# K and V in transfers of four heads, long weight rows, bf16 transposes, output in rows and w2 last: one decode layer on one core

## The chip, the core and the metric

The kernel runs on one core of a Trainium2 chip. Five engines work beside each other, each through its own list of instructions in order: PE (TensorE, matmuls; its weight loads are shown as PEld), DVE (VectorE), ACT (ScalarE), POOL (GpSimd) and SP (SyncE, which here only issues transfers). Sixteen DMA engines move data between HBM and SBUF; PE writes its results to PSUM, from where DVE or ACT copies them. The metric is device time in microseconds (us): the median of several runs. The kernel before takes 142.29 us (three runs, 142.29 to 142.35).

## The reference

A parallel layer for one new token and a batch of two (D = 576). The normalized input goes both through attention over the last 2048 of 8192 cached positions (32 query heads of width 128, 16 heads in the K and V caches, so two query heads share one) and through a dense block with squared ReLU (F = 4608); both results are added to the input.

```python
W = min(4096, max(256, Sk // 4))                       # 2048
q = (x @ wq).reshape(B, 1, 32, 128)
k = jnp.repeat(k_cache[:, :, Sk - W:, :], 2, axis=1)
v = jnp.repeat(v_cache[:, :, Sk - W:, :], 2, axis=1)
p = softmax(einsum(q, k) * 128 ** -0.5)
attn = einsum(p, v).reshape(B, 1, 4096) @ wo
h = xn @ w1 + b1
mlp = where(h > 0, h, 0) ** 2 @ w2 + b2
out = x + attn(xn) + mlp(xn)                           # xn = layernorm(x)
```

All inputs and the output are bf16. K and V of the window are 33.55 MB, wq and wo 4.72 MB each, w1 and w2 5.31 MB each: 53.6 MB are read, and hardly anything is written.

## The kernel before

**Tiles.** K and V come one head of one batch at a time, 512 KB each: `kv_view` (L80) puts 16 consecutive positions into each of the 128 partitions, so a row of a transfer is 4 KB. `issue_wo` (L140) loads two heads' 256 rows of wo with rows of 1152 bytes, and `issue_w2` (L154) 512 rows of w2, mostly as rows of 4608 bytes. wq and w1 come in pieces of 128 rows of 8192 and 9216 bytes, with a remainder of 64 rows folded over all partitions.

**Steps.** The main loop (L407) has 16 steps, one per K/V head, for both batches. `transposes` (L295) views pairs of bf16 columns as f32 and turns them with 8 f32 matmuls of 128 columns against an identity; ACT copies one half of the result to SBUF and DVE the other. Since the pairs are still interleaved after that, the query is first spread into `zq` with a zero in every second place (L280 to L289), and `scores` (L315) makes two accumulating matmuls for each pair. `softmax` (L325) takes the maximum over positions (DVE, then POOL across partitions), subtracts, exponentiates (ACT), sums (DVE, POOL) and inverts. `pv` (L352) runs two steps later, `wo_proj` (L366) three steps later. The output is built transposed: each block of 128 rows of wo or w2 is the stationary operand in five column blocks, with two moving columns (the batch), and all add up in one PSUM tile, `outT_ps`. At the end x and b2 are added (L452), five transposes bring the result into rows (L455), and it is copied and stored.

**Order.** All loads are issued by SP in program order. A list of eight semaphores is used in turn, so the ninth transfer waits for the first to land; beyond that a transfer waits until its buffer is free (ten K and ten V buffers). w1 is loaded in the first steps, w2 and wo are spread over the steps, and the last loads are V of heads 14 and 15, a w2 piece, and wo of heads 13 to 15. Inside a step PE runs transposes, the older `pv`, `scores` of one batch, `wo_proj`, the dense block's matmuls, and `scores` of the other batch; a framework places the waits and shifts some of these.

**Start.** The identities are made on POOL (`make_identity`, lines of `masks.py`), behind four small transfers that POOL issues itself.

Of the kernel before, what the change touches and what calls it, by code (L numbers as in the profile page):

```python
# [9 lines left out]
F32 = mybir.dt.float32  # L10
# [7 lines left out]
def kernel(  # L18
# [50 lines left out]
    ktpool = ctx.enter_context(tc.tile_pool(name="ktpool", bufs=5))  # L69
    wbig = ctx.enter_context(tc.tile_pool(name="wbig", bufs=NFULL))  # L70
    wrem = ctx.enter_context(tc.tile_pool(name="wrem", bufs=2))
    wpool = ctx.enter_context(tc.tile_pool(name="wpool", bufs=3))
    wopool = ctx.enter_context(tc.tile_pool(name="wopool", bufs=6))
    work = ctx.enter_context(tc.tile_pool(name="work", bufs=3))
    keep = ctx.enter_context(tc.tile_pool(name="keep", bufs=5))
# [5 lines left out]
    def kv_view(cache, b, t):  # L81
        return cache[b, t, S0:Sk, :].rearrange("(p j) d -> p j d", p=P)

    k_tiles, v_tiles, wq_tiles, w1_tiles, wo_tiles, w2_tiles = {}, {}, {}, {}, {}, {}
    WBW = max(Hq * Dh, F)

    def issue_k(t, b):
        tl = kpool.tile([P, NJ, Dh], BF16, tag="k_sb", name=f"k_{t}_{b}")
        nc.sync.dma_start(out=tl[:], in_=kv_view(A_k_cache, b, t))
        k_tiles[(t, b)] = tl  # L90

    def issue_v(t, b, pool=None):
        if pool is None:
            tl = vpool.tile([P, NJ, Dh], BF16, tag="v_sb", name=f"v_{t}_{b}")
        else:
            tl = pool.tile([P, NJ, Dh], BF16, tag="k_sb", name=f"v_{t}_{b}")
        nc.sync.dma_start(out=tl[:], in_=kv_view(A_v_cache, b, t))
        v_tiles[(t, b)] = tl

    WRW = max(LQ, L1)  # L100

    def issue_wq(c):
        if c < NFULL:
            tl = wbig.tile([P, WBW], BF16, tag="wbig", name=f"wq_{c}")
            nc.sync.dma_start(out=tl[:, 0:Hq * Dh], in_=A_wq[c * P:(c + 1) * P, :])
        else:
            tl = wrem.tile([P, WRW], BF16, tag="wrem", name="wq_rem")
            nc.sync.dma_start(out=tl[:, 0:LQ],
                              in_=A_wq[NFULL * P:D, :].rearrange("r (s l) -> (r s) l", s=S))
        wq_tiles[c] = tl  # L110

    def issue_w1(c):
        if c < NFULL:
            tl = wbig.tile([P, WBW], BF16, tag="wbig", name=f"w1_{c}")
            nc.sync.dma_start(out=tl[:, 0:F], in_=B_w1[c * P:(c + 1) * P, :])
        else:
            tl = wrem.tile([P, WRW], BF16, tag="wrem", name="w1_rem")
            nc.sync.dma_start(out=tl[:, 0:L1],
                              in_=B_w1[NFULL * P:D, :].rearrange("r (s l) -> (r s) l", s=S))
        w1_tiles[c] = tl  # L120
# [9 lines left out]
    GW = FG * P  # L130

    def piece_permuted(g):
        return (g * GW) // L1 == (g * GW + GW - 1) // L1

    def h_cols(fc):
        g, r = divmod(fc, FG)
        if piece_permuted(g):
            return g * GW + r, FG
        return g * GW + r * P, 1

    def issue_wo(t, split=False):
        h0 = rep * t
        if not split:
            tl = wopool.tile([P, rep, D], BF16, tag="wo_sb", name=f"wo_{t}")
            nc.sync.dma_start(out=tl[:],
                              in_=A_wo[h0 * Dh:(h0 + rep) * Dh, :].rearrange("(r p) n -> p r n", p=P))
            for hh in range(rep):
                wo_tiles[h0 + hh] = (tl, hh)
        else:
            for hh in range(rep):  # L150
                tl = wopool.tile([P, 1, D], BF16, tag="wo_sb", name=f"wo_{t}_{hh}")
                nc.sync.dma_start(out=tl[:, 0, :], in_=A_wo[(h0 + hh) * Dh:(h0 + hh + 1) * Dh, :])
                wo_tiles[h0 + hh] = (tl, 0)

    def issue_w2(m):
        tl = wpool.tile([P, FG, D], BF16, tag="w2_sb", name=f"w2_{m}")
        rows = B_w2[m * GW:(m + 1) * GW, :]
        if piece_permuted(m):
            nc.sync.dma_start(out=tl[:], in_=rows.rearrange("(p r) n -> p r n", r=FG))
        else:  # L160
            nc.sync.dma_start(out=tl[:], in_=rows.rearrange("(r p) n -> p r n", p=P))
        w2_tiles[m] = tl
# [6 lines left out]
    nc.scalar.activation(out=warm[:, 0:1], in_=eps_t[:], func=ACT.Sqrt)  # L169
    issue_wq(0)  # L170
    issue_k(0, 0)
    b1_sb = const.tile([NFC, P], BF16, name="b1_sb")
    nc.gpsimd.dma_start(out=b1_sb[:], in_=B_b1.rearrange("(c p) -> c p", p=P))  # L173
    b1g_sb = const.tile([NMG, GW], BF16, name="b1g_sb")
    nc.gpsimd.dma_start(out=b1g_sb[:], in_=B_b1.rearrange("(g c) -> g c", c=GW))
    b2_sb = const.tile([NCH, OC], BF16, name="b2_sb")
    nfull = D // OC
    nc.gpsimd.dma_start(out=b2_sb[0:nfull, :], in_=B_b2[0:nfull * OC].rearrange("(c p) -> c p", p=OC))
    for c in range(nfull, NCH):
        nc.gpsimd.dma_start(out=b2_sb[c:c + 1, :],  # L180
                            in_=B_b2[ostart[c]:ostart[c] + OC].rearrange("(c p) -> c p", c=1))
    issue_wq(1)
    issue_k(0, 1)
    issue_wq(2)
    issue_k(1, 0)
    issue_wq(3)
    issue_k(1, 1)
    for c in range(4, KC):
        issue_wq(c)

    ident = const.tile([P, P], BF16, name="ident")
    make_identity(nc, ident[:])
    ident_f = const.tile([P, P], F32, name="ident_f")
    make_identity(nc, ident_f[:])
    HP = P // 2
    sel = const.tile([P, 2, P], BF16, name="sel")
    nc.gpsimd.memset(sel[:], 0.0)
    for i in range(2):
        nc.gpsimd.affine_select(
            out=sel[:, i, :].rearrange("p (a u) -> p a u", a=2),  # L200
            in_=sel[:, i, :].rearrange("p (a u) -> p a u", a=2),
            compare_op=ALU.not_equal, fill=1.0, base=-i,
            pattern=[[0, 2], [-2, HP]], channel_multiplier=1,
        )

    outT_ps = psum.tile([OC, NCH, B], F32, tag="outT", name="outT_ps")
    nc.vector.memset(outT_ps[:], 0.0)
# [14 lines left out]

# [5 lines left out]
    NXN = NFULL + S  # L228
    OFF_XN = 0
    OFF_X = OFF_XN + NXN * B  # L230
    PRO_W = OFF_X + NCH * B
    pro_ps = psum.tile([P, PRO_W], BF16, tag="misc", name="pro_ps")
    for c in range(NFULL):
        nc.tensor.transpose(out=pro_ps[:, OFF_XN + c * B:OFF_XN + (c + 1) * B],  # L234
                            in_=xn_sb[:, c * P:(c + 1) * P], identity=ident[:B, :B])
    for sg in range(S):
        c = NFULL + sg
        nc.tensor.transpose(out=pro_ps[:, OFF_XN + c * B:OFF_XN + (c + 1) * B],
                            in_=xr_sb[:, sg, :], identity=ident[:B, :B])
    for c in range(NCH):  # L240
        nc.tensor.transpose(out=pro_ps[:OC, OFF_X + c * B:OFF_X + (c + 1) * B],
                            in_=x_sb[:, ostart[c]:ostart[c] + OC], identity=ident[:B, :B])
    OFF_PB2 = NFC
    OFF_PBP = NFC + NCH + 1
    NMGP = NMG + (NMG % 2)
    pb_ps = psum.tile([P, OFF_PBP + FG * NMGP], BF16, tag="oT", name="pb_ps")
    nc.tensor.transpose(out=pb_ps[:, 0:NFC], in_=b1_sb[:], identity=ident[:NFC, :NFC])
    nc.tensor.transpose(out=pb_ps[:OC, OFF_PB2:OFF_PB2 + NCH], in_=b2_sb[:], identity=ident[:NCH, :NCH])
    for r in range(FG):
        nc.tensor.transpose(out=pb_ps[:, OFF_PBP + r * NMGP:OFF_PBP + r * NMGP + NMG],  # L250
                            in_=b1g_sb[:, r::FG], identity=ident[:NMG, :NMG])
# [3 lines left out]
    b1T = const.tile([P, NMG, FG], F32, name="b1T")
    nc.vector.tensor_copy(out=b1T[:].rearrange("p g r -> p r g"),
                          in_=pb_ps[:, OFF_PBP:OFF_PBP + FG * NMGP].rearrange("p (r g) -> p r g", r=FG)[:, :, 0:NMG])
    for g in range(NMG):
        if not piece_permuted(g):
            nc.vector.tensor_copy(out=b1T[:, g, :], in_=pb_ps[:, g * FG:(g + 1) * FG])  # L260
# [229 lines left out]
```

## Time and profile before

| | us |
|---|---|
| median of three runs | 142.29 |
| span of the profiled execution | 140.5 |
| PE busy (matmuls) | 103.5 |
| DVE busy | 41.3 |
| ACT busy | 42.6 |
| POOL busy | 17.1 |

The profiled execution's own time is 142.29 us, its span 140.5 us, so 1.8 us lie around the span. The page gives the busy time of each engine, then the span in 40 slices of 3.5 us with a digit for each (busy tenths), the clock that was granted to TensorE in tenths (PEclk), and the busy share and rate of the DMA engines. The main queue, q1, holds all loads that SP issues. The groups of instructions have busy time, the mean length of one in ns, and the idle time before them with what ended it. A matmul's length there contains its way through the array; the distance from one to the next is much shorter.

### The profile page before, as it was taken

The numbers are of one execution on the slowest core, as the hardware profiler recorded it, in microseconds if no ns is written. First come the engines' busy times: TensorE is split into PE (matmuls) and PEld (weight loads), VectorE is DVE, ScalarE is ACT, GpSimd is POOL, SyncE is SP. The second block draws the span as 40 slices with busy tenths as digits, with TensorE's granted clock in tenths as the row PEclk, the third lists the DMA queues.
The fourth block names the chain that finished last, engine by engine and source line by source line (L and its number), as shares of the span: only waits on it lengthen the run. The fifth ranks groups of instructions, "written<-read, shape, count | busy, mean of one in ns | idle before, by whom it ended". The sixth has DMA issues, their size and how long they took to land.

```text
span 140.5 us, 4501 instructions
## 1 busy us (share of the span) xinstructions
PE 103.5 (74%) x1984; PEld 100.3 (71%) x1984; DVE 41.3 (29%) x137; ACT 42.6 (30%) x57; POOL 17.1 (12%) x47
## 2 busy tenths in 40 slices
PE   0000699889939999999996947969696969696461
PEld 0000699879829999999996947968696959696451
DVE  4200213425622324324232321323141413232001
ACT  6600024256603341523320502323231405050000
POOL 6100300001330102020111020111101020202000
PEclk9999999999995959585555685557777865555555
DMA  4999999999999999999999999999999999999930
GB/s 131 417 415 415 418 411 404 412 411 408 408 411 430 396 414 406 405 430 394 405 407 405 412 402 406 410 403 407 395 410 410 405 412 401 411 410 407 382 122 1
DMA packets 16859, 53.92 MB, mean 384 GB/s; under 512 B 1711, under 2 KB 6344, under 8 KB 15816
## 3 DMA queue, kind: packets, MB, share of 16 engines
q1 hardware_dynamic: 16708, 53.62, 96.2%
q8 instruction: 15, 0.25, 0.7%
q0 software_dynamic: 128, 0.02, 0.1%
q14 instruction: 4, 0.03, 0.1%
q10 hardware_dynamic: 4, 0.00, 0.0%
HBM read 53.63 MB, written 0.00 MB: 382 GB/s over the span
## 4 chain that ended last, share of the span: by engine, by line
DMA 56%; PE 24%; issue 9%; POOL 4%; DVE 3%; ACT 0%; POOLq 0%; SPq 0%
DMA w<-in_B_w_dram 22%; PE kT_ps L305 15%; DMA v<-in_A_v_cache_dram 15%; DMA k<-in_A_k_cache_dram 14%; DMA wo<-in_A_wo_dram 5%; PE qT_ps L276 3%; PE sc_ps L321 2%; DVE kT L311 1%; PE oT_ps L358 1%; POOL lsum L343 1%; PE hT_ps L383 1%; POOL b_sb L173 1%; PE outT_ps L371 1%; POOL gmax L330 1%; PE fin_ps L455 1%
## 5 line engine op out<-in xcount | busy, mean ns | idle before, releaser
L305 PE MATMUL kT_ps<-ident_f,k 128*128 128x128 f32 x256 | 56.0, 404 | 8.9 <-DMA k<-in_A_k_cache_dram 8.6
L305 PEld LDWEIGHTS kT_ps<-ident_f,k 128*128 128x128 f32 x256 | 49.1, 216 | 10.4 <-issue 9.0
L309 ACT COPY kT<-kT_ps 128x1024 bf16<-128x1024 bf16 x32 | 32.4, 1012 | 55.7 <-PE kT_ps L305 55.7
L311 DVE COPY kT<-kT_ps 128x1024 bf16<-128x1024 bf16 x32 | 22.1, 691 | 43.0 <-PE kT_ps L305 43.0
L358 PE MATMUL oT_ps<-pT,v 128*128 128x2 bf16 x512 | 17.6, 164 | 5.5 <-DVE oTn L361 3.7
L358 PEld LDWEIGHTS <-v 128*128 128x128 bf16 x512 | 15.6, 100 | 5.8 <-DMA v<-in_A_v_cache_dram 3.1
L321 PE MATMUL sc_ps<-zq,kT 128*128 128x4 bf16 x512 | 17.9, 166 | 0.5 <-ACT zq L289 0.5
L321 PEld LDWEIGHTS <-kT 128*128 128x128 bf16 x512 | 17.6, 102 | 0.7
L330 POOL PARTITION_ALL_REDUCE gmax<-m x16 | 6.0, 373 | 83.3 <-DVE m L327 83.3
L338 ACT ACTIVATE pT<-sub 128x64 bf16<-128x64 f32 x16 | 4.1, 257 | 26.5 <-DVE sub L334 26.5
L234 PE MATMUL pro_ps<-ident,xn_sb 2*128 2x2 bf16 x4 | 0.2, 160 | 15.3 <-POOL ident masks.py:199 15.3
L234 PEld LDWEIGHTS <-xn_sb 2*128 2x128 bf16 x4 | 0.3, 100 | 15.2 <-issue 8.6
L343 POOL PARTITION_ALL_REDUCE lsum<-l x16 | 6.9, 437 | 16.5 <-DVE l L340 16.5
L401 PE MATMUL outT_ps<-hT_sb,w 128*128 128x2 bf16 x180 | 6.0, 165 | 2.9 <-DMA w<-in_B_w_dram 1.5
L401 PEld LDWEIGHTS <-w 128*128 128x128 bf16 x180 | 5.4, 100 | 3.3 <-DMA w<-in_B_w_dram 2.2
L371 PE MATMUL outT_ps<-oTn,wo 128*128 128x2 bf16 x160 | 6.2, 165 | 0.3 <-DMA wo<-in_A_wo_dram 0.2
L334 DVE TENSOR_TENSOR sub<-sc_ps,gmax 128x64 f32<-128x64 f32 x16 | 3.6, 224 | 8.4 <-POOL gmax L330 8.4
L327 DVE TENSOR_REDUCE m<-sc_ps 128x4 f32<-128x64 f32 x16 | 3.6, 222 | 8.2 <-PE sc_ps L321 8.2
L371 PEld LDWEIGHTS <-wo 128*128 128x128 bf16 x160 | 5.3, 101 | 0.5 <-DMA wo<-in_A_wo_dram 0.5
L347 DVE RECIPROCAL rinv<-lsum 128x4 f32<-128x4 f32 x16 | 2.8, 178 | 9.5 <-POOL lsum L343 9.5
L383 PE MATMUL hT_ps<-xnT,w 128*128 128x2 bf16 x144 | 5.2, 171 | 0.0
L383 PEld LDWEIGHTS <-w 128*128 128x128 bf16 x144 | 5.0, 115 | 0.0
(66 smaller groups left out, 38.4 us busy)
## 6 DMA issues: line engine op xcount, KB each, us to landing
k<-in_A_k_cache_dram SPq DMA_DIRECT2D x32, 512.0 KB, 10.6
v<-in_A_v_cache_dram SPq DMA_DIRECT2D x32, 512.0 KB, 10.4
w<-in_B_w_dram SPq DMA_DIRECT2D x9, 576.0 KB, 10.0
w<-in_B_w_dram SPq DMA_DIRECT2D x4, 1152.0 KB, 12.7
wo<-in_A_wo_dram SPq DMA_DIRECT2D x15, 288.0 KB, 9.5
wq<-in_A_wq_dram SPq DMA_DIRECT2D x4, 1024.0 KB, 7.9
w_rem<-in_B_w_dram SPq DMA_DIRECT2D x1, 576.0 KB, 11.3
wq_rem<-in_A_wq_dram SPq DMA_DIRECT2D x1, 512.0 KB, 14.0
```

The lines of the kernel that those rows point to most:

```text
L276: nc.tensor.matmul(qT_ps[:, h, :], lhsT=lhsT, rhs=xnT[:, xc, :], start=False, stop=False, skip_group_check=True)
L305: nc.tensor.transpose(out=kT_ps[:, q, :], in_=srcv, identity=ident_f[:])
L309: nc.scalar.copy(out=dst, in_=psb)
L311: nc.vector.tensor_copy(out=dst, in_=psb)
L321: nc.tensor.matmul(sc_ps[:, b, 2 * pp:2 * pp + 2, :], lhsT=kTp[:, pp, :, i], rhs=zq[:, i, b, t, :, :], start=(i == 0), stop=(i == 1))
L330: nc.gpsimd.partition_all_reduce(gmax[:].rearrange("p b h -> p (b h)"), m1[:].rearrange("p b h -> p (b h)"), channels=P, reduce_op=ReduceO ...
L338: nc.scalar.activation(out=pT[:], in_=sub[:], func=ACT.Exp, scale=scale)
L343: nc.gpsimd.partition_all_reduce(lsum[:].rearrange("p b h -> p (b h)"), l1[:].rearrange("p b h -> p (b h)"), channels=P, reduce_op=ReduceO ...
L358: nc.tensor.matmul(oT_ps[:, b, :], lhsT=v_sb[:, j, :], rhs=pT[:, b, j, :], start=(j == 0), stop=(j == NJ - 1))
L371: nc.tensor.matmul(outT_ps[:, c, :], lhsT=wo_sb[:, r, ostart[c]:ostart[c] + OC], rhs=oTn[:, hh, :], start=False, stop=False, skip_group_ch ...
L383: nc.tensor.matmul(hT_ps[:, fc, :], lhsT=lhsT, rhs=xnT[:, xc, :], start=False, stop=False, skip_group_check=True)
L401: nc.tensor.matmul(outT_ps[:, c, :], lhsT=w2_sb[:, i, ostart[c]:ostart[c] + OC], rhs=hT_sb[:, fc, :], start=False, stop=False, skip_group_ ...
```

## The change

Nothing of what is computed changes. The arrangement does, in nearly every part:

- **K and V** come in eight units of four heads of one batch, 2 MB each: partition 4c + h holds 64 consecutive positions of head h (`unit_view`), so a row of a transfer is 16 KB. Unit 0 of K comes in two halves of 8 KB rows, between the first pieces of wq. K, V and later w2 share six buffers of 2 MB (`kvpool`).
- **Masked softmax.** Since a partition belongs to one of four heads, the scores are computed for all eight query heads of the unit, and a large offset (`offm`) sends the six query heads that do not belong to the partition to zero through the exponential. `scores` and `pv` have eight moving columns; the softmax chain works on 128x512 values eight times, instead of on 128x64 values sixteen times, with two small DVE operations more.
- **Transposes** are bf16, 512 in place of 256, eight to a PSUM buffer; copies are as many and as large as before, alternately on ACT and DVE. `zq` and its two selection matmuls fall away.
- **Output in rows.** `out_acc` makes two matmuls for each block of 128 rows of wo or w2: the stationary operand has two columns (the batch), the moving one 288 columns of the weight, and the halves go to PSUM partitions 0 and 32. x and b2 are added by matmuls at the start. `wo_proj` comes four times: since wo is loaded with eight consecutive rows per partition (9216 bytes), the attention output is first regrouped by one DVE product, eight matmuls against a selection matrix and a DVE copy.
- **w1 and w2** are paired with a hidden layer in an order that makes rows of w2 long (18 consecutive rows per partition, loaded 9, 9, 9, 6 and 3 at a time); w2 is the last load and the last work.
- **Start.** The identity is made on DVE, from a running sum and a 32x32 transpose.

The core of the diff:

```diff
-    kpool = ctx.enter_context(tc.tile_pool(name="kpool", bufs=10))
-    vpool = ctx.enter_context(tc.tile_pool(name="vpool", bufs=10))
+    kvpool = ctx.enter_context(tc.tile_pool(name="kvpool", bufs=6))
...
+    def unit_view(cache, u):
+        tq, b = divmod(u, B)
+        return cache[b, tq * TH:(tq + 1) * TH, S0:Sk, :].rearrange("h (c j) d -> c h (j d)", c=CP)
...
+    def issue_wo(tq):
+        tl = wopool.tile([P, WR, D], BF16, tag="wo_sb", name=f"wo_{tq}")
+        n = NC * Dh
+        nc.sync.dma_start(out=tl[:], in_=A_wo[tq * n:(tq + 1) * n, :].rearrange("(p r) n -> p r n", r=WR))
...
+    def issue_w2(s, r0, r1):
+        tl = kvpool.tile([P, (r1 - r0) * D], BF16, tag="kv", name=f"w2_{s}_{r0}")
+        rows = B_w2[s * L1:(s + 1) * L1, :].rearrange("(p r) n -> p (r n)", r=FR)
+        nc.sync.dma_start(out=tl[:], in_=rows[:, r0 * D:r1 * D])
...
+    def out_acc(lhsT, rhs_of, start=False, stop=False):
+        for i in range(2):
+            nc.tensor.matmul(out_ps[32 * i:32 * i + B, :], lhsT=lhsT, rhs=rhs_of(i * OH, (i + 1) * OH),
+                             start=start, stop=stop, skip_group_check=True)
...
+        for i in range(JG):
+            j = g * JG + i
+            nc.tensor.transpose(out=kT_ps[:, i * P:(i + 1) * P], in_=k_sb[:, j * Dh:(j + 1) * Dh], identity=ident[:])
...
+    def wo_proj(tq):
+        oG = oG_tiles.pop(tq)
+        rr = work.tile([P, WR, NC * B], BF16, tag="rr", name=f"rr_{tq}")
+        nc.vector.tensor_tensor(
+            out=rr[:],
+            in0=oG[:].rearrange("p h b -> p (h b)").unsqueeze(1).to_broadcast([P, WR, NC * B]),
+            in1=rmask[:].unsqueeze(2).to_broadcast([P, WR, NC * B]), op=ALU.mult)
+        wps = psum.tile([P, WR, B], F32, tag="misc", bufs=2, name=f"wps_{tq}")
+        for h in range(NC):
+            nc.tensor.matmul(wps[:], lhsT=sel[:, h, :, :].rearrange("p a c -> p (a c)"),
+                             rhs=rr[:, :, h * B:(h + 1) * B], start=(h == 0), stop=(h == NC - 1))
+        ws = work.tile([P, WR, B], BF16, tag="ws", name=f"ws_{tq}")
+        nc.vector.tensor_copy(out=ws[:], in_=wps[:])
+        wo_sb = wo_tiles.pop(tq)
+        for r in range(WR):
+            out_acc(ws[:, r, :], lambda a, z: wo_sb[:, r, a:z])
...
+    W2P = [(0, 0, 9), (0, 9, 18), (1, 0, 9), (1, 9, 15), (1, 15, 18)]
...
+    for u in range(2, NU + 2):
+        if u < NU:
+            step(u)
+        else:
+            for g in range(NG):
+                pv(u - 2, g)
...
+    for i, w in enumerate(W2P):
+        mlp_o(*w, last=(i == len(W2P) - 1))
```

The end of the list of SP, in the kernel before (k_14_0 is K of head 14, batch 0; wo_14 is wo of head pair 14; the brackets name the semaphores of a wait, DMAHW those of earlier transfers, PE those of the matmuls that free a buffer):

```order
L97 DMA v_14_0_2141<-in_A_v_cache_dram 128x2048 [waits DMAHW4_49]
L97 DMA v_14_1_2143<-in_A_v_cache_dram 128x2048 [waits DMAHW5_49]
L97 DMA v_15_0_2145<-in_A_v_cache_dram 128x2048 [waits DMAHW6_49]
L97 DMA v_15_1_2147<-in_A_v_cache_dram 128x2048 [waits DMAHW7_49]
L159 DMA w2_8_2149<-in_B_w2_dram 128x2304 [waits DMAHW0_49,PE_49]
L145 DMA wo_13_2151<-in_A_wo_dram 128x2x576 [waits DMAHW1_49]
L145 DMA wo_14_2291<-in_A_wo_dram 128x2x576 [waits DMAHW2_49]
L152 DMA wo_15_0_2431<-in_A_wo_dram 128x576 [waits DMAHW3_49,PE_49]
L152 DMA wo_15_1_2433<-in_A_wo_dram 128x576 [waits DMAHW4_49,PE_49]
```

And in the changed kernel (k_7 is K of unit 7, w2_0_9 the piece of w2 that begins at row 9 of its first half):

```order
L94 DMA k_7_1906<-in_A_k_cache_dram 128x1x8192 [waits DMAHW5_49,DMAHW4_49,PE_49]
L94 DMA v_6_2146<-in_A_v_cache_dram 128x1x8192 [waits DMAHW6_49,PE_49]
L123 DMA wo_3_2148<-in_A_wo_dram 128x4608 [waits PE_49]
L94 DMA v_7_2416<-in_A_v_cache_dram 128x1x8192 [waits DMAHW7_49,PE_49]
L129 DMA w2_0_0_2418<-in_B_w2_dram 128x5184 [waits DMAHW0_49,PE_49]
L129 DMA w2_0_9_2420<-in_B_w2_dram 128x5184 [waits DMAHW2_49,DMAHW1_49,PE_49]
L129 DMA w2_1_0_2422<-in_B_w2_dram 128x5184 [waits DMAHW3_49,PE_49]
L129 DMA w2_1_9_2424<-in_B_w2_dram 128x3456 [waits DMAHW4_49,PE_49]
L129 DMA w2_1_15_2426<-in_B_w2_dram 128x1728 [waits DMAHW5_49,PE_49]
```

Behind the last K there are now 10.7 MB in eight transfers, of which the last five, half of the bytes, are w2; every one of them waits for a buffer that PE frees.

The list of DVE behind the last unit's copies, in the changed kernel; in the kernel before, the same place holds only the chain of one head (L327 to L347), three products oTn, the sum with x and b2 and one copy:

```order
L258 TENSOR_REDUCE m1_7_2369<-sc_ps_7_2200 128x8
L260 TENSOR_TENSOR m2_7_2371<-m1_7_2369,offm_146 128x8
L264 TENSOR_TENSOR gm2_7_2375<-gmax_7_2373,offm_146 128x8
L266 TENSOR_TENSOR sub_7_2377<-sc_ps_7_2200,gm2_7_2375 128x512
L294 TENSOR_TENSOR oG_3_2493<-oT_ps_6_2428,rinv_6_2144 128x8
L271 TENSOR_REDUCE l1_7_2381<-pT_7_2379 128x8
L275 RECIPROCAL rinv_7_2385<-lsum_7_2383 128x8
L294 TENSOR_TENSOR oG_3_2493<-oT_ps_7_2495,rinv_7_2385 128x8
L300 TENSOR_TENSOR rr_3_2561<-oG_3_2493,rmask_148 128x128
L309 CAST ws_3_2572<-wps_3_2563 128x16
L414 CAST fin_sb_2662<-out_ps_162 34x288
```

Between the last scores and the last use of wo stand two large DVE operations, two passes over POOL, and the regrouping (rr, ws) with eight matmuls on PE between them; behind that only w2 and one copy are left.

More of the change, by code (lines that the diff above doesn't have):

```diff
@@ L255 @@
[L255 to L260, printed above, removed]
-    b2T = const.tile([OC, NCH], F32, name="b2T")
-    nc.vector.tensor_copy(out=b2T[:], in_=pb_ps[:OC, NFC:NFC + NCH])
@@ L365, in wo_proj @@
[L365 to L372 removed]
+        l1 = work.tile([P, NC], F32, tag="l1", name=f"l1_{u}")
+        nc.vector.tensor_reduce(out=l1[:], in_=pT[:].rearrange("p j c -> p c j"), axis=AX.X, op=ALU.add)
@@ L451 @@
-    resT = work.tile([OC, NCH, B], BF16, tag="resT", name="resT")
-    nc.vector.tensor_tensor(out=resT[:], in0=outT_ps[:], in1=xb2T[:], op=ALU.add)
-    fin_ps = psum.tile([B, D], BF16, tag="misc", name="fin_ps")
-    for c in range(NCH):
-        nc.tensor.transpose(out=fin_ps[:, ostart[c]:ostart[c] + OC], in_=resT[:, c, :],
-                            identity=ident[:OC, :OC])
-    fin_sb = work.tile([B, D], BF16, tag="fin", name="fin_sb")
-    nc.vector.tensor_copy(out=fin_sb[:], in_=fin_ps[:])
@@ L459, with mlp_o, load_k, load_v @@
-    nc.sync.dma_start(out=out2d, in_=fin_sb[:])
+            mlp["h"] = hT_sb
+    def mlp_o(s, r0, r1, last=False):
+        w2_sb = w2_tiles.pop((s, r0))
+        for r in range(r0, r1):
+            o = (r - r0) * D
+            out_acc(mlp["h"][:, s * FR + r, :], lambda a, z: w2_sb[:, o + a:o + z], stop=(last and r == r1 - 1))
+    def load_k(u):
+        for f in issue_kv(k_tiles, A_k_cache, u, "k"):
+            f()
+    def load_v(u):
+        for f in issue_kv(v_tiles, A_v_cache, u, "v"):
+            f()
@@ new lines, with step @@
+    W2P = [(0, 0, 9), (0, 9, 18), (1, 0, 9), (1, 9, 15), (1, 15, 18)]
+    load_k(1)
+    issue_w1(0)
+    issue_w1(1)
+    load_v(0)
+    load_k(2)
+    for c in range(2, KC):
+        issue_w1(c)
+    load_v(1)
+    issue_wo(0)
+    load_k(3)
+    nxt = {0: [], 1: [], 2: [lambda: load_v(2), lambda: load_k(4)]}
+    def step(u, extra=()):
+        for g in range(NG + 2):
+            if g < NG:
+                transposes(u, g)
+            if u >= 1 and 1 <= g <= NG:
+                if u >= 2:
+                    pv(u - 2, g - 1)
+            if g >= 2:
+                scores(u, g - 2)
+        softmax(u)
```

484 lines of the change are left out of this document (188 added, 296 removed).

## The prediction

> **What bounds the kernel now.** I read the slices first, then the queues, then the end of the chain of waits. Slices and queue:
>
> ```profile
> PEclk9999999999995959585555685557777865555555
> DMA  4999999999999999999999999999999999999930
> DMA packets 16859, 53.92 MB, mean 384 GB/s; under 512 B 1711, under 2 KB 6344, under 8 KB 15816
> q1 hardware_dynamic: 16708, 53.62, 96.2%
> k<-in_A_k_cache_dram SPq DMA_DIRECT2D x32, 512.0 KB, 10.6
> ```
>
> The DMA engines are full from the first slice to the last but one, and a load waits 10.6 us from issue to landing, so there is always a queue. The kernel is bound by its transfers: only their bytes, their rate, and what lies before the first and behind the last byte count. The end of the chain, and three windows (us, busy by engine, PEclk, DMA share, GB/s):
>
> ```profile
> 129.08 7.38 DMA wo<-in_A_wo_dram
> 136.50 0.31 PE outT_ps L371 x5
> 136.83 0.18 DVE resT L452
> 137.06 0.71 PE fin_ps L455 x5
> 137.79 0.44 DVE fin_sb L458
> 136.08:136.50 0.42, 0.35 (x10) 0.23 (x7) 0.00 (x0) 0.00 (x0) 0.00 (x0) 0.50 0.00 0
> 138.23:140.50 2.27, 0.00 (x0) 0.00 (x0) 0.00 (x1) 0.00 (x0) 0.00 (x0) 0.50 0.00 1
> ```
>
> From 136.08 no load is moving, 0.42 us later PE has the last wo, 1.73 us go to five matmuls, sum, transposes and copy, and 2.27 us to the store. So 134.3 us of loads (from about 1.75) and a tail of 4.42 us.
>
> **The loads.** Bytes are the same, rows are longer. The rate by row length comes from windows with known contents: in 4:16 pieces of wq (8 KB rows) and K (4 KB) alternate, two bytes to one; in 20:32 there are K and V alone; in 100:104 about half are rows of wo (1152 bytes).
>
> ```profile
> 4.00:16.00 12.00, 0.69 (x17) 0.73 (x17) 1.02 (x5) 1.85 (x4) 0.97 (x5) 1.00 1.02 419
> 20.00:32.00 12.00, 10.92 (x192) 10.43 (x191) 4.04 (x11) 5.23 (x7) 0.39 (x1) 1.00 1.03 408
> 100.00:104.00 4.00, 4.00 (x40) 3.96 (x40) 1.07 (x2) 2.02 (x2) 0.00 (x0) 0.58 1.06 395
> ```
>
> 4 KB rows run at 408 GB/s, 160.6 ns for each of 16 rows at a time; taking their third out of 419 leaves 425 for 8 KB, 308.7 ns. A straight line through both gives 12.5 ns per row plus 148.1 ns per 4 KB. On it 16 KB rows reach 433, 9216 bytes 427, 1152 bytes 340; the half of window 100:104 that is wo says 380. I take 428 for 16 KB, between the 425 seen and the 433 drawn on, and 360 for 1152.
>
> K and V: 33.55 MB / 408 = 82.2 us; after, 31.46 MB / 428 + 2.10 / 425 = 78.4, so 3.8 us less. wo: 4.72 / 360 = 13.1 to 4.72 / 427 = 11.1, 2.0 less (1.4 to 2.8). w2 (one of nine pieces had 1152 byte rows, the others 4608): 0.7 less. wq and w1 are unchanged. Sum 6.5 us, so the loads end at 129.6. Bounds: 433 and 340 give 127.9; if K and V gain nothing, 133.4.
>
> Do the six buffers stop the queue? Most transfers ask for a buffer that was freed three units back. With the PE times below, the tightest are the last two w2 pieces: they ask for buffers that PE frees at 116.4 and 118.1, and the queue reaches them at 126.4 and 128.5. Eight us of cover; if PE were later than that, each further us would be paid. Start: identity on DVE instead of
>
> ```profile
> 14.97 0.29 POOL ident masks.py:199
> ```
>
> lets PE begin with unit 0 about 7 us earlier. That gives nothing by itself, since the queue is full either way.
>
> **PE.** It is no longer certain that it keeps up, so its work is costed too. The rows (timelines: start, length; the windows as above):
>
> ```profile
> 17.40 1.89 PE L276 MATMUL qT_ps<-xnT,wq 128*128 128x2 bf16 x64
> 29.08 1.09 PE L305 MATMUL kT_ps<-ident_f,k 128*128 128x128 f32 x4
> 36.23 0.63 PE L305 MATMUL kT_ps<-ident_f,k 128*128 128x128 f32 x4
> 99.97:103.38 3.41, 3.38 (x16) 3.41 (x17) 0.69 (x1) 1.51 (x2) 0.00 (x0) 0.50 1.05 393
> 103.38:106.80 3.42, 2.69 (x96) 2.47 (x93) 1.36 (x4) 0.77 (x2) 0.64 (x2) 1.00 1.04 412
> 113.60:117.00 3.40, 2.37 (x11) 2.40 (x12) 0.63 (x3) 1.01 (x1) 0.43 (x1) 0.50 1.02 404
> 117.00:120.40 3.40, 3.40 (x92) 3.33 (x92) 1.25 (x4) 1.01 (x1) 0.37 (x1) 0.50 1.04 410
> ```
>
> A short matmul with its own weights takes 27 ns. Sixteen f32 transposes fill 3.38 us at clock 0.5, 211 ns each; four take 1.09 us there and 0.63 at clock 1, about half per matmul. The clock opens after a stretch of 3.4 us full of transposes (99.97, then 1.0) and not after one with eleven (113.6); when a stretch of short matmuls follows, it falls again. The five bf16 transposes of 128 columns at 137.06 take 0.71 us, with a length of 0.31 for one, so about 105 ns each: half an f32 one. Two of these replace one f32, 512 x 105 = 54 us against 56 now: no change, provided that loading K as weights stays hidden, as it is behind the f32 stream (weight loads are busy beside the matmuls for all of 99.97:103.38). That is the first unknown: 0 or 27 ns each; I take 0.
>
> Scores and pv stay at 27 ns with eight columns. A matmul of `out_acc` streams 288 columns: 105 x 288 / 128 = 236 ns at clock 0.5, 119 at 1. The two of a pair write different partitions and sit in different columns of the array. No matmul here does so; a pair costs one stream (236) or two (472). I take one, because neither half needs the other's columns, and keep two for the range. The Trainium skill ("TensorEngine Tiling", Key Properties) says that different tiles can execute weight load and matmul in parallel, which is the first; no run here shows it yet.
>
> DVE, ACT and POOL stay beside: a unit has eight copies as now, and its chain grows with 512 columns:
>
> ```profile
> L309 ACT COPY kT<-kT_ps 128x1024 bf16<-128x1024 bf16 x32 | 32.4, 1012 | 55.7 <-PE kT_ps L305 55.7
> L311 DVE COPY kT<-kT_ps 128x1024 bf16<-128x1024 bf16 x32 | 22.1, 691 | 43.0 <-PE kT_ps L305 43.0
> L330 POOL PARTITION_ALL_REDUCE gmax<-m x16 | 6.0, 373 | 83.3 <-DVE m L327 83.3
> L338 ACT ACTIVATE pT<-sub 128x64 bf16<-128x64 f32 x16 | 4.1, 257 | 26.5 <-DVE sub L334 26.5
> L327 DVE TENSOR_REDUCE m<-sc_ps 128x4 f32<-128x64 f32 x16 | 3.6, 222 | 8.2 <-PE sc_ps L321 8.2
> ```
>
> Copies show 0.49 ns (DVE) and 0.79 ns (ACT) per column more; for f32 I double the first. So maximum and subtraction 0.67 us each, exponential 0.61, two small steps 0.1 each, POOL 0.37, handoffs 0.4: 3.0 us from scores to pT (estimate).
>
> A unit costs PE 64 x (105 + 27) = 8.5 us for transposes and scores at clock 0.5, 5.0 at 1, 1.7 for pv, and half a wo_proj, about 2.1: 12.3 cold, against 11.2 for its transfers (4.19 MB / 428 + 1.18 / 427 / 2). It is therefore near a tie, with the clock as judge. The end: K of unit 7 lands 10.7 MB (25.0 us) before the last byte, at 104.7, and K of unit 6 at 94.9. Unit 6 to 105.1 (cold), wo_proj 2.4 for its chain and 1.9 for eight pairs, 109.4. Unit 7: 5 us cold until the clock opens, 2 us open, 116.4; pv of unit 6 to 118.1; pT at 119.4; pv to 121.1; sum, product, regrouping 1.7; wo 1.9: 124.7. Then 36 pairs of w2: 8.5 us cold, 133.2; with the clock open 5 us into this streaming, 130.5. The transfers alone would give 129.6 + 0.42 + three pairs 0.7 = 130.7. I take 131.8, halfway between 130.5 and 133.2.
>
> **Sum.** 131.8 + latency 0.2 (at 136.50 five short matmuls take 0.31, of it four distances of 0.027) + handoff 0.03 + copy of 288 columns 0.33 (between 0.22 for 64 and 0.44 for 576) + 2.27 = 134.6 of span, against 140.5. Around the span lie 1.8 us (142.29 - 140.5; the median is 142.29 too): **136.4 us**.
>
> **Rivals.**
>
> 1. *16 KB rows are worth no more than 4 KB rows.* For: nothing longer than 9216 bytes runs here; against: 408 to 425 on one doubling. Loads end at 133.4, tail 0.42 + 0.7 + 2.83: span 137.3, time 139.1.
> 2. *The halves of `out_acc` stream one behind the other.* For: every matmul of this trace does. Then wo_proj 1.9 longer twice, and 72 matmuls of w2: wo ends at 128.5, clock opens at 129.7, PE ends at 137.7; span 140.5, time 142.3 (cold to the end, 150).
> 3. *Slower: weight loads of K are not hidden*, and PE becomes the bound. Place: between two transposes of `transposes`; price 27 ns x 64 = 1.7 us per unit, so a unit takes 14.0 cold against 11.2. Five units lag by up to 14; one opened stretch per unit gives back about 1.1 of the 2.8; 8.5 us on the end: span 143, time 145. It turns slower than before from about 18 ns per transpose (5.9 us over 5 x 64). Against: the f32 rows; for: bf16 streams half as long per load. The Trainium skill ("TensorE: Matmul & The Clock Gate", Back-to-back issue gap) gives about 81 ns for such pairs at 128 columns against 56 alone at the full clock; by it this rival's 25 ns would be the rule, while the f32 rows show no such addition.
> 4. *Slower transfers.* Neighbouring partitions now read places 2 MiB apart. If this cost as much as the slowest full window above, 393 GB/s for K and V, 80.1 + 4.9 = 85.0 us, the loads end at 136.2, time 141.9; any worse is slower than before. For it: only the new stride; against: w1 and wq with their strides of 8 to 9 KB ran best. The Trainium skill ("DMA: Bandwidth & Descriptors", Latency and other measured facts) has 164 against 214 GB/s for rows 2 MiB apart, which on K and V would be some 27 us; here only every fourth row makes such a step, and no run shows it.
>
> **How the numbers follow.** Forecast 56%, rival 1 12%, 2 15%, 3 10%, 4 7%. What this kernel's measurement can tell from no change is about 0.2%, 0.3 us. Faster than 142.0 are the forecast, rival 1, a third of 2 and some of 3: 76%; within 0.3 us part of 2: 5%; slower 19%. The range: below, loads end at 127.9 and PE never late, 127.9 + 0.42 + 0.4 + 2.83 + 1.8 = 133.3; above, it takes in rivals 1, most of 2 and half of 3: 133.0 to 145.0. The forecast's own is 133.3 to 139.
>
> **What would show it.** Right: about 427 GB/s in the middle slices, loads at an end near 130, transposes 105 or 53 ns apart, 36 pairs in less than 9 us, last matmul within 2 us of the last byte. Wrong: idle slices of DMA (buffers), PE busy 9 in each slice with loads finished long before the end, matmuls of a pair one after the other.

## The result, and the profile after

The changed kernel takes 137.4 us (median of four runs, 137.19 to 137.44) against 142.32 in the runs of the kernel before beside it: a ratio of 0.9653, 95% interval 0.9639 to 0.9667. The forecast was 136.4. (Times and ratios below leave out slow executions, which only the run with both halves of a pair in the same columns had: two of ten.) The profiled span went from 140.5 to 135.6 us.

From the page of the changed kernel: the slices, the queues, and one row of the issues.

```profile
PEclk9999985569855685556985698698559959955599
DMA  5999999999999999999999999999999999999940
DMA packets 5278, 53.90 MB, mean 397 GB/s; under 512 B 630, under 2 KB 652, under 8 KB 1164
q1 hardware_dynamic: 5188, 53.61, 94.7%
v<-in_A_v_cache_dram SPq DMA_DIRECT2D x8, 2048.0 KB, 28.4
```

The bytes are the same, the packets a third, and the DMA engines are still full from the first slice to the last but one. The kernel is bound by its transfers as before. Two stretches of each kernel (us, busy by engine, PEclk, DMA share, GB/s), the kernel before first:

```profile
16.00:128.00 112.00, 97.56 (x1842) 95.14 (x1840) 37.42 (x118) 37.93 (x51) 12.82 (x33) 0.72 1.03 408
133.00:136.20 3.20, 2.16 (x68) 1.96 (x69) 0.16 (x1) 0.00 (x0) 0.00 (x0) 0.50 0.50 176
```

and the changed one:

```profile
16.00:128.00 112.00, 91.10 (x1889) 82.78 (x1888) 47.46 (x97) 35.87 (x39) 6.10 (x16) 0.71 1.01 423
128.50:131.80 3.30, 2.21 (x36) 1.34 (x32) 0.00 (x0) 0.00 (x0) 0.00 (x0) 1.00 0.52 204
```

The full stretch runs at 423 GB/s and no longer at 408. Some 47.9 MB move after 16 us (53.6 MB less 16 us at 355 GB/s, as both kernels have it): 117.5 us at the one rate, 113.3 at the other, so 4.2 us. Each kernel then ends its loads with some 3 us in which the DMA engines are half empty. At the full rate all would have landed at 133.5 and 129.3; it landed at 136.1 and 131.8. That loss of about 2.5 us is common to both and drops out of the difference. So the loads end 4.3 us earlier, and 0.6 us is saved behind them: 3.8 us from the last byte to the end, where there were 4.4.

The end of the changed kernel, first on the chain of waits, then in the timeline of PE (start, length, work, and in brackets the idle time before it with what ended it):

```profile
119.21 13.05 DMA w<-in_B_w_dram
132.30 0.55 PE out_ps L213 x6
132.87 0.45 DVE fin_sb L414
```

```profile
97.31 2.74 PE L237 MATMUL kT_ps<-ident,k 128*128 128x128 bf16 x24 [2.29 <-DMA k<-in_A_k_cache_dram]
101.16 0.61 PE L237 MATMUL kT_ps<-ident,k 128*128 128x128 bf16 x8
109.80 2.22 PE L237 MATMUL kT_ps<-ident,k 128*128 128x128 bf16 x24
122.83 2.08 PE L213 MATMUL out_ps<-wo,ws 128*2 128x288 bf16 x16 [0.27 <-DVE ws L309]
124.70 4.18 PE L213 MATMUL out_ps<-w,hT_sb 128*2 128x288 bf16 x36
129.16 1.27 PE L213 MATMUL out_ps<-w,hT_sb 128*2 128x288 bf16 x18 [0.28 <-DMA w<-in_B_w_dram]
131.24 0.90 PE L213 MATMUL out_ps<-w,hT_sb 128*2 128x288 bf16 x12 [0.81 <-DMA w<-in_B_w_dram]
132.30 0.53 PE L213 MATMUL out_ps<-w,hT_sb 128*2 128x288 bf16 x6 [0.17 <-DMA w<-in_B_w_dram]
```

PE is never the bound: it waits for K of unit 6 (2.29 us) and for each of the last three pieces of w2 (1.26 us together). But it has little to spare: without those three waits its last matmul would end at about 131.6, as against 132.8.

### The profile page after: what moved, and what is told of

Its sections match the earlier page's. It is cut to its first block, busy times and chain, and to the rows that moved or that the text cites. A ratio compares the mean times of both kernels' runs of the same rounds, so it can differ in the third digit from the quotient of the medians.

```text
span 135.6 us, 4461 instructions
## 1 busy us (share of the span) xinstructions
PE 102.5 (76%) x2054; PEld 91.9 (68%) x2054; DVE 53.9 (40%) x124; ACT 43.0 (32%) x47; POOL 10.0 (7%) x31
## 4 chain that ended last, share of the span: by engine, by line
DMA 55%; PE 35%; DVE 3%; issue 2%; POOL 1%; ACT 1%; SPq 1%; POOLq 0%; ACTq 0%
DMA k<-in_A_k_cache_dram 41%; PE kT_ps L237 18%; DMA w<-in_B_w_dram 10%; PE hT_ps L323 5%; DMA b_sb<-in_B_b_dram 4%; PE sc_ps L252 4%; PE out_ps L213 4%; PE oT_ps L289 3%; PE qT_ps L225 1%; ACT kT L240 1%; POOL b_sb L146 1%; DVE l L271 1%; DVE sub L266 1%; SPq L94 0%; DVE fin_sb L414 0%
## 5 line engine op out<-in xcount | busy, mean ns | idle before, releaser
L237 PE MATMUL kT_ps<-ident,k 128*128 128x128 bf16 x512 | 47.3, 260 | 9.9 <-DMA k<-in_A_k_cache_dram 9.9
L237 PEld LDWEIGHTS <-k 128*128 128x128 bf16 x512 | 39.6, 119 | 11.8 <-DMA k<-in_A_k_cache_dram 10.7
L252 PE MATMUL sc_ps<-qT_all,kT 128*128 128x8 bf16 x512 | 21.6, 168 | 1.6 <-ACT kT L240 0.8
L289 PE MATMUL oT_ps<-pT,v 128*128 128x8 bf16 x512 | 15.5, 167 | 1.9 <-issue 1.4
L269 ACT ACTIVATE pT<-sub 128x512 bf16<-128x512 f32 x8 | 5.0, 630 | 35.1 <-DVE sub L266 35.1
L271 DVE TENSOR_REDUCE l<-pT 128x8 f32<-128x512 bf16 x8 | 8.5, 1066 | 4.2 <-ACT pT L269 4.2
L213 PE MATMUL out_ps<-wo,ws 128*2 128x288 bf16 x64 | 8.3, 438 | 2.4 <-DVE ws L309 2.4
L258 DVE TENSOR_REDUCE m<-sc_ps 128x8 f32<-128x512 f32 x8 | 5.5, 692 | 9.7 <-PE sc_ps L252 9.7
L213 PE MATMUL out_ps<-w,hT_sb 128*2 128x288 bf16 x72 | 6.9, 353 | 1.3 <-DMA w<-in_B_w_dram 1.3
L266 DVE TENSOR_TENSOR sub<-sc_ps,gm 128x512 f32<-128x512 f32 x8 | 5.5, 692 | 0.3
## 6 DMA issues: line engine op xcount, KB each, us to landing
v<-in_A_v_cache_dram SPq DMA_DIRECT2D x8, 2048.0 KB, 28.4
k<-in_A_k_cache_dram SPq DMA_DIRECT2D x7, 2048.0 KB, 29.4
```

Source lines behind the costliest of these rows:

```text
L213: nc.tensor.matmul(out_ps[32 * i:32 * i + B, :], lhsT=lhsT, rhs=rhs_of(i * OH, (i + 1) * OH), start=start, stop=stop, skip_group_check=True)
L237: nc.tensor.transpose(out=kT_ps[:, i * P:(i + 1) * P], in_=k_sb[:, j * Dh:(j + 1) * Dh], identity=ident[:])
L252: nc.tensor.matmul(sc_ps[:, g * JG + i, :], lhsT=kT[:, i * P:(i + 1) * P], rhs=qT_all[:, b, tq * NC:(tq + 1) * NC], start=True, stop=True)
L258: nc.vector.tensor_reduce(out=m1[:], in_=sc_ps[:].rearrange("p j c -> p c j"), axis=AX.X, op=ALU.max)
L266: nc.vector.tensor_tensor(out=sub[:], in0=sc_ps[:], in1=gm2[:].unsqueeze(1).to_broadcast([P, NJ, NC]), op=ALU.subtract)
L269: nc.scalar.activation(out=pT[:], in_=sub[:], func=ACT.Exp, scale=scale)
```

## The experiments

All start from the changed kernel (137.4); ratios are to the kernel before, measured beside each.

### K and V in shorter rows

The number of column parts of each K and V transfer is raised to four; in the second run to two, for all but the first K, which had two already.

```diff
-        for f in issue_kv(k_tiles, A_k_cache, u, "k"):
+        for f in issue_kv(k_tiles, A_k_cache, u, "k", parts=4):
-        for f in issue_kv(v_tiles, A_v_cache, u, "v"):
+        for f in issue_kv(v_tiles, A_v_cache, u, "v", parts=4):
```

> The changed kernel, but each K and V unit comes in four transfers of 4 KB rows instead of one of 16 KB. Theory (the row length makes the rate, 408 against 428 GB/s): 3.8 us back, about 141.2 us. Rival (the gain came from elsewhere, from the tail or from PE's earlier start): no change, 137.4 us.

Measured: 140.77 us, ratio 0.9893 (0.9878 to 0.9908). The full stretch of this run:

```profile
16.00:128.00 112.00, 89.43 (x1856) 81.19 (x1856) 47.37 (x97) 35.35 (x38) 6.10 (x16) 0.73 1.02 411
```

411 instead of 423 GB/s, the last byte at 135.1 instead of 131.8: the rows of 16 KB are worth 3.3 us of loads. The run also makes four transfers out of one. With each transfer go sixteen packets of 4 bytes; the trace has 1367 of them in place of 615, at 9 ns each, so that some 0.4 us of the 3.3 can come from the number of transfers (estimate). A row of 4 KB takes 163 ns here, a row of 16 KB 622 ns in the changed kernel, or 155 for each 4 KB.

> The changed kernel with K and V units in two transfers of 8 KB rows. By the straight line (308.7 ns for 8 KB, 605 for 16 KB) 0.7 to 1.5 us more than the changed kernel, 138.1 to 138.9 us; if the gain of row length ends at 8 KB, 137.4 us.

Measured: 139.54 us, ratio 0.9806 (0.9792 to 0.9821). The last byte comes at 133.0, 1.2 us later, and the end another 0.9 us behind. The second part has a cause of its own. PE in this run:

```profile
110.41 0.36 PE L306 MATMUL wps<-rr,sel 128*128 128x16 bf16 x8 [4.34 <-DVE rr L300]
128.28 6.01 PE L213 MATMUL out_ps<-w,hT_sb 128*2 128x288 bf16 x72
```

and DVE in this run, over the same place:

```profile
105.31 0.69 DVE L258 TENSOR_REDUCE m<-sc_ps 128x8 f32<-128x512 f32 x1 [0.69 <-PE sc_ps L252]
...
108.35 1.05 DVE L271 TENSOR_REDUCE l<-pT 128x8 f32<-128x512 bf16 x1 [0.69 <-ACT pT L269]
109.32 0.16 DVE L294 TENSOR_TENSOR oG<-oT_ps,rinv 128x8 bf16<-128x8 f32 x1
110.00 0.20 DVE L275 RECIPROCAL rinv<-lsum 128x8 f32<-128x8 f32 x1 [0.52 <-POOL lsum L273]
110.12 0.24 DVE L300 TENSOR_TENSOR rr<-oG,rmask 128x128 bf16<-128x128 bf16 x1
```

The product oG of unit 5, on which wo_proj waits, stands here behind the softmax of unit 6 on DVE. In the changed kernel it stands ahead of most of it:

```profile
105.34 0.69 DVE L258 TENSOR_REDUCE m<-sc_ps 128x8 f32<-128x512 f32 x1 [0.87 <-PE sc_ps L252]
105.97 0.17 DVE L294 TENSOR_TENSOR oG<-oT_ps,rinv 128x8 bf16<-128x8 f32 x1
106.07 0.17 DVE L260 TENSOR_TENSOR m<-m,offm 128x8 f32<-128x8 f32 x1
106.17 0.29 DVE L300 TENSOR_TENSOR rr<-oG,rmask 128x128 bf16<-128x128 bf16 x1
```

There rr starts at 106.17 and not at 110.12. In this run PE then goes through all 72 matmuls of w2 with no wait: it, and no longer the transfer, ends last. The same order stood in this run before the wo_proj of units 2 and 3, where PE waited 3.8 us for rr (0.6 in the changed kernel). That is how near PE is to the bound: delays of some 4 us, twice, show in the time. The run with four parts has this order too (a wait of 3.7 us for the rr of unit 5), but there the loads end later, at 135.1, and hide it. No run changes the order alone.

### The 2 MiB steps of the addresses

Each unit reads one contiguous 2 MB instead of rows of four heads 2 MiB apart (other keys and values, so other outputs).

```diff
-        return cache[b, tq * TH:(tq + 1) * TH, S0:Sk, :].rearrange("h (c j) d -> c h (j d)", c=CP)
+        return cache[b, tq * TH + (u % TH), :, :].rearrange("(p j) d -> p (j d)", p=P)
```

> The changed kernel, but each unit is read from 2 MB that lie in one piece in HBM (8192 positions of one head) instead of four heads 2 MiB apart: other data, so the output is another; rows, bytes and order are the same. If the steps of 2 MiB cost nothing: 137.4 us. If they cost as the fourth rival has it (393 GB/s or worse): 5 us or more faster.

Measured: 137.47 us, ratio 0.9664 (0.9649 to 0.9678):

```profile
16.00:128.00 112.00, 92.11 (x1882) 84.70 (x1880) 47.48 (x97) 36.12 (x39) 6.10 (x16) 0.70 1.01 423
```

The same 423 GB/s. The steps cost nothing here. The Trainium skill's 164 against 214 GB/s ("DMA: Bandwidth & Descriptors", Latency and other measured facts) is for copies between HBM tensors with every row 2 MiB from the last. In the changed kernel three of four rows lie 2 MiB behind the one before, and the fourth goes back to the first head (partition 4c + h holds head h); the prediction's "every fourth row" is wrong. Still no run here shows a loss.

### wo in short rows, w2 in short rows, all of them

```diff
-        ... A_wo[tq * n:(tq + 1) * n, :].rearrange("(p r) n -> p r n", r=WR))
+        ... A_wo[tq * n:(tq + 1) * n, :].rearrange("(r p) n -> p r n", r=WR))
```

> The changed kernel, but wo is loaded in rows of 1152 bytes (eight blocks of 128 rows) as before; its rows then meet the wrong attention outputs, so the output is another. Theory: 2.0 us back (1.4 to 2.8), 139.4 us. Rival (short rows are hidden by other transfers): no change.

Measured: 139.51 us, ratio 0.9805 (0.9789 to 0.9821), the last byte at 133.8, so 2.0 us later. (The rows of wo meet other rows of the product, so the output is another.)

```diff
-        nc.sync.dma_start(out=tl[:], in_=rows[:, r0 * D:r1 * D])
+        for a in range(r0, r1, 4):
+            z = min(a + 4, r1)
+            nc.sync.dma_start(out=tl[:, (a - r0) * D:(z - r0) * D], in_=rows[:, a * D:z * D])
```

> w2 alone goes back to short rows: each piece is loaded in steps of four rows of 1152 bytes (4608 bytes in one) and a rest of one to three (1152 to 3456). The loads ended at 131.8 us and not at 129.6, so one of the three gains forecast was too large, or they do not add. If w2's long rows are worth the 0.7 us of the sum, 138.1. If they are worth nothing, 137.4, and 0.7 of the missing 2.2 us lay here.

Measured: 137.96 us, ratio 0.9698 (0.9684 to 0.9711): 0.6 us in the time, and the last byte at 132.2, 0.4 us later. The last run has both edits and K and V in four parts.

> K and V in rows of 4096 bytes, wo in rows of 1152, w2 as in the run with w2 alone: all three back to short rows, in the order of the changed kernel. One at a time, K and V cost 3.4 us and wo 2.1. If the gains add, the loads end at 131.8 + 3.3 + 2.1 + (0 to 0.7) = 137.2 to 137.9 and the time is 142.9 to 143.6. If they do not add, the loads end where those of the kernel before did, at 136.1, and the time is 141.7: then the terms were each about right and their sum was not.

Measured: 143.3 us, ratio 1.0075 (1.0062 to 1.0088): slower than the kernel before. The three gains add: the loads end 3.3 + 2.0 + 0.4 = 5.7 us later, at 137.5. With all rows short the changed kernel does not fall back to the old time but passes it by 1.0 us. Three stretches of this run, the first whole, the second while wo is loaded, the third its end:

```profile
16.00:128.00 112.00, 88.34 (x1836) 80.16 (x1838) 46.75 (x96) 34.24 (x37) 6.10 (x16) 0.73 1.03 402
68.00:70.00 2.00, 0.26 (x10) 0.17 (x7) 1.30 (x2) 0.63 (x1) 0.00 (x0) 0.50 1.05 365
134.50:137.50 3.00, 1.84 (x22) 0.94 (x22) 0.00 (x0) 0.00 (x0) 0.00 (x0) 1.00 0.54 211
```

402 GB/s where the kernel before had 408, and loads that end at 137.5, 1.4 us later than there. The sizes of the rows are nearly the same in both (only w2's rests are cut otherwise); what differs is their order. In the kernel before, wo came in pieces of 288 KB between pieces of K and V: 395 GB/s in 100 to 104 us, half of it wo by the packets of the trace. Here it comes 1152 KB at a time: 365 to 378 in four stretches of 2 us, about two thirds of them wo. With the rest at 408, that says 383 GB/s for wo between other rows and 357 for wo in a block, and on 4.72 MB 0.9 us (estimate). So the order of wo carries most of the 1.4 us; the rest is open, and the places of w2's pieces changed too.

### Two halves of an output pair

The second half of a pair goes to the same partitions and the same columns of the array as the first, so that its sum is added to the first half's.

```diff
-            nc.tensor.matmul(out_ps[32 * i:32 * i + B, :], lhsT=lhsT, ...
+            nc.tensor.matmul(out_ps[0:B, :], lhsT=lhsT, ...
```

> The changed kernel, but both halves of out_acc write the same partitions, so that their weights sit in the same columns of the array (the second half's result is lost in the first's, the output is another). Theory (the halves stream side by side only because they use different columns): the second rival's time, 142.3 us (PE ends 5.9 us later), with 120 to 238 ns between the matmuls of a pair instead of 4. Rival (they would overlap anyway): 137.4 us.

Measured: 142.16 us, the median of eight runs (141.44 to 143.54), ratio 0.9998 (0.9962 to 1.0034). The loads still end at 131.8. PE at the end of this run:

```profile
125.45 4.00 PE L213 MATMUL out_ps<-wo,ws 128*2 128x288 bf16 x16 [0.27 <-DVE ws L309]
129.25 9.71 PE L213 MATMUL out_ps<-w,hT_sb 128*2 128x288 bf16 x72
```

Eight pairs take 4.00 us here and 2.08 in the changed kernel, so that there a pair costs one stream. (The edit moves both the columns and the PSUM partitions of the second half; which of the two makes the halves wait is not separated.) PE is the bound, as in rival 2. The Trainium skill ("TensorEngine Tiling (Array Packing)", Key Properties) says that different tiles can work in parallel; 2.08 against 4.00 us agrees.

### f32 transposes

Each transpose takes two bf16 columns as one f32 again, half as many of them (columns of K are interleaved, so scores stand in another order).

```diff
-        for i in range(JG):
-            j = g * JG + i
-            nc.tensor.transpose(... in_=k_sb[:, j * Dh:(j + 1) * Dh], identity=ident[:])
+        for i in range(JG // 2):
+            j = g * JG + 2 * i
+            nc.tensor.transpose(... in_=k_sb[:, j * Dh:(j + 2) * Dh].bitcast(F32), identity=ident_f[:])
```

> The changed kernel with f32 transposes, four of 128 columns per group instead of eight in bf16; the columns then come out interleaved, so scores and output are others. Theory (one f32 transpose streams as long as two bf16, and both hide their weight loads): no change, 137.4 us within 0.4. Rival (bf16 gained something on PE): up to 2 us slower; (bf16 lost something): faster.

Measured: 137.38 us, ratio 0.9661 (0.9647 to 0.9675). 256 transposes of 50.0 us busy, for 512 of 47.3:

```profile
L239 PE MATMUL kT_ps<-ident_f,k 128*128 128x128 f32 x256 | 50.0, 349 | 9.4 <-DMA k<-in_A_k_cache_dram 9.4
```

The form of the transpose is worth nothing in the time.

### w2 not last

V of the last unit is loaded behind w2, and PE does w2 before it.

```diff
-            load_v(u)
+            if u < NU - 1:
+                load_v(u)
...
             for w in W2P:
                 issue_w2(*w)
+            load_v(u)
...
```

> The changed kernel, but V of the last unit is loaded behind w2, and the w2 matmuls come before its pv. The bytes end when they ended (131.8 us of the profiled span); behind them stand 64 matmuls of pv 1.7, product and regrouping 1.6, eight pairs of wo 2.0 instead of three pairs 0.5. Theory (w2 last shortens what stands behind the last byte): 4.6 us more, 142.0 us. Rival (that order is worth nothing): 137.4 us.

Measured: 142.03 us over ten runs, ratio 0.9982 (0.9973 to 0.9991). The loads end at 131.8 as before; behind them stand now, on the chain of waits:

```profile
118.49 13.73 DMA v<-in_A_v_cache_dram
132.27 1.88 PE oT_ps L289 x64
...
135.35 2.10 PE out_ps L213 x16
```

4.6 us for what is loaded last, as much as all three sorts of long rows brought between the two kernels (4.3). It is no part of the gain over the kernel before: there too only wo and a piece of w2 came behind the last V, with 4.4 us behind the last byte against 3.8 now. It is what the changed kernel would lose with V at the end.

### The half-empty end

Two attempts to shorten the last 3 us. First, the rows of the last piece are dealt out to the engines in another way (source split in 8 by 16, so that rows land on other partitions and the output is another).

```diff
+        if r1 - r0 == 3:
+            nc.sync.dma_start(out=tl[:], in_=rows[:, r0 * D:r1 * D].rearrange("(q a) n -> a q n", a=8))
...
```

> The changed kernel, but the last w2 piece (442 KB) is loaded with its source split eight times sixteen, so that only eight of the sixteen DMA engines can carry it (its rows then meet the wrong hidden values, the output is another). At the end of the changed kernel the DMA share is 0.54 for 3.2 us, as if eight engines were through and eight were late. If the eight that carry the piece are the early ones: 1.0 us faster, 136.4 us. If they are the late ones: 1.0 us slower, 138.4 us. If the late engines are mixed among both: about 1 us slower.

Measured: 140.3 us, ratio 0.9861 (0.9843 to 0.9879): 2.9 us slower, which none of the expectations had. The last byte comes at 134.6. The split made the transfer itself slow: its rows of 3456 bytes take 209 ns in the mean (143 in the changed kernel), those of the piece before it 349 (266), and from 132.0 to 134.5 us the DMA share is 0.14, as if some two engines of sixteen were at work. So it says nothing on which engines are late; inconclusive. Second, the last two pieces of w2 are cut 8 + 1 rows instead of 6 + 3.

```diff
-    W2P = [(0, 0, 9), (0, 9, 18), (1, 0, 9), (1, 9, 15), (1, 15, 18)]
+    W2P = [(0, 0, 9), (0, 9, 18), (1, 0, 9), (1, 9, 17), (1, 17, 18)]
```

> The last two pieces of w2 are cut 8 + 1 rows instead of 6 + 3. In the changed kernel PE waits for the last piece and then has three pairs left, 0.53 us. With one pair left about 0.24 us less (two pairs of 0.12 us): 137.1. If the end of the loads moves instead because the rows are cut otherwise, up to 0.3 us either way around that.

Measured: 137.65 us, ratio 0.9677 (0.9664 to 0.969), 0.25 slower and not 0.24 faster. PE at its end:

```profile
129.01 1.27 PE L213 MATMUL out_ps<-w,hT_sb 128*2 128x288 bf16 x18 [1.56 <-DMA w<-in_B_w_dram]
131.80 1.27 PE L213 MATMUL out_ps<-w,hT_sb 128*2 128x288 bf16 x18 [1.52 <-DMA w<-in_B_w_dram]
```

The wait has moved to the larger piece ahead: PE gets both pieces, nine pairs, in one go at 131.80. By the packets of the trace the last row of the larger piece lands at 131.2 and that of the smaller one at 131.6 (130.7 and 131.8 in the changed kernel), so the smaller last piece leaves more, not less, behind the last wait. (0.25 us lies within the 0.3 that the expectation left for a moved end of the loads.)

### Four buffers

```diff
-    kvpool = ctx.enter_context(tc.tile_pool(name="kvpool", bufs=6))
+    kvpool = ctx.enter_context(tc.tile_pool(name="kvpool", bufs=4))
```

> Four buffers for K, V and w2 instead of six. The prediction had about 8 us between the time a buffer is free and the time the queue reaches it, at the tightest place. Each buffer less takes away one transfer, about 5 us: with four the cover is gone and some 2 us are paid, 139.4. If PE is never that late (the changed kernel's K and V wait 28 us in the queue from issue to landing), nothing is lost: 137.4.

Measured: 137.29 us, ratio 0.9651 (0.9638 to 0.9665): nothing lost. From issue to landing in this run:

```profile
v<-in_A_v_cache_dram SPq DMA_DIRECT2D x8, 2048.0 KB, 20.4
k<-in_A_k_cache_dram SPq DMA_DIRECT2D x7, 2048.0 KB, 17.2
```

A transfer waits some 10 us less in the queue (28.4 and 29.4 us in the changed kernel), and the stretch from 16 to 128 us still runs at 423 GB/s. So the 8 us of cover with six buffers were too low an account.

## Why the prediction was right

The sign and the cause hold, and the time is 1.0 us above the forecast; that it is no more is partly luck, as the fifth point says. Point by point:

- **The loads end at 131.8, not at 129.6.** This is the step that failed: 6.5 us of gain, of which 4.3 came. The largest part is the term for wo. It was priced with rows of 1152 bytes at 360 GB/s. That is near the 357 of wo in a block, and against such blocks long rows do save 2.0 us; but the kernel before did not have those blocks, and its order was 1.4 us better than the changed one's at equal rows. Of the 2.0 us, 1.1 is left if the estimated 0.9 belongs to wo, and 0.6 if all of the 1.4 does. The row that was at hand, 395 GB/s for a window half of wo, meant 380 and a gain of 1.4, the lower bound. K and V gave 3.3 of 3.8: the full stretch runs at 423 GB/s with 16 KB and 9 KB rows mixed, below the 428 taken. w2 gave 0.4 of 0.7. In sum 3.3 + 2.0 + 0.4 - 1.4 = 4.3.
- **Half-empty end.** It was inside the 134.3 us from which the sum subtracts, and it is as long after as before, so that it did no harm to the sum, though the prediction did not see it.
- **PE.** The weight loads of K stay hidden: 24 transposes in 2.74 us are 107 ns apart at clock 0.5 and 8 in 0.61 are 55 at clock 1, as forecast (105 and 53). So rival 3 falls. The Trainium skill's 81 ns for such pairs ("TensorE: Matmul & The Clock Gate", Back-to-back issue gap) is not what this trace has. The halves of a pair stream together: 2.08 us for eight pairs (forecast 1.9), 4.00 without it. Rival 2 falls, and the run that makes it true gives 142.16 (142.3 forecast).
- **The dates of the last units.** Unit 7 starts at 109.80 (109.4 forecast), wo ends at 124.9 (124.7). The chain from scores to pT takes 3.0 us (maximum at 105.34, sum over pT from 108.39), as estimated, with maximum and subtraction at 0.69 and the exponential at 0.63.
- **The end.** 131.8 for PE alone was halfway between two bounds, with no working behind the middle; its own work would have ended at 131.6. The forecast had PE last, by 1.1 us over the transfers. In fact the transfers are last and PE 1.2 us ahead. Therefore 2.2 us of missing gain cost only 1.0 us of time, and that is luck: a slow PE was forecast where the loads turned out slow. Behind the last matmul 2.77 us follow (2.8 forecast).
- **Costed at nothing, and nothing:** transposes in bf16 (137.38), buffers (137.29 with four). The earlier start of PE was not tried by itself; since PE waits 9.9 us for K in the changed kernel, it should give nothing.

```profile
PE kT_ps L237 <- DMA k<-in_A_k_cache_dram: 9.9, 4, 4.3
```

- **Rivals 1 and 4.** Rows of 16 KB beat rows of 4 KB by 3.3 us; the 2 MiB steps cost nothing, although they are three times as frequent as the prediction has them. (The 27 us that the prediction works out from the ratio of 164 to 214 come out as 24 to 25, on 78.4 or 82.2 us of loads.)

Of the 4.9 us of span, the loads gave 4.3, at 423 GB/s in place of 408 (5.7 for longer rows, less 1.4 for their order), and the shorter end 0.6. That w2 comes last is what keeps the end short: the forecast counts it only in its tail, and the run without it shows that 4.6 us hang on it.

## What to carry to other kernels

In a kernel bound by its transfers, read the rate of a row length from a window in which those rows stand in the order that they really have: short rows between longer ones cost less than a block of them, and a gain priced from a block is too large. What is loaded last should be what needs least behind it; here the wrong choice would have cost as much as the rate brought. And a second engine that is 1 us ahead of the transfers is a second bound: a reordering on DVE of some 4 us showed in the run whose loads ended early enough.

## What the runs showed of the hardware that was not expected

- The last 3 us of the loads run at half capacity: 0.50 of the DMA engines in the kernel before, with wo in rows of 1152 bytes at the end, 0.52 in the changed one with w2, and 0.52 to 0.56 in the runs with contiguous units, with four parts and with all rows short. It costs about 2.5 us in both kernels, and neither attempt shortened it. The sixteen engines are not abreast there: in the changed kernel the first row of the last piece starts at 127.3, while rows of the piece ahead of it move until 130.7. Which engines lag, and why, is open.
- Stretches with two thirds of their bytes in blocks of 1152-byte rows run at 365 to 378 GB/s; half and half with rows of 4 KB between them, 395.
- A sum over 512 bf16 columns in eight groups of 64 takes longer than the maximum over the same number of f32 columns in PSUM:

```profile
L271 DVE TENSOR_REDUCE l<-pT 128x8 f32<-128x512 bf16 x8 | 8.5, 1066 | 4.2 <-ACT pT L269 4.2
L258 DVE TENSOR_REDUCE m<-sc_ps 128x8 f32<-128x512 f32 x8 | 5.5, 692 | 9.7 <-PE sc_ps L252 9.7
```

It lies behind pT and delays nothing here.

- The w1 matmuls now take their weights from every 18th column instead of (nearly always) every fourth, and the same 144 of them are busy for longer. In the changed kernel:

```profile
L323 PE MATMUL hT_ps<-xnT,w 128*128 128x2 bf16 x144 | 9.8, 201 | 0.0
```

and in the kernel before:

```profile
L383 PE MATMUL hT_ps<-xnT,w 128*128 128x2 bf16 x144 | 5.2, 171 | 0.0
```

That the stride is the cause was not tried; the 4.6 us are off the path, since PE waits for K afterwards.
